# Turning normed tiles with VectorE and a scratch tensor instead of TensorE in a chunk-attention and Fourier-mixing kernel

## The chip, the cores and the metric

The kernel runs on one core of one Trainium2 chip. TensorE (PE in the profile) multiplies, and also transposes by a product with an identity matrix; VectorE (DVE), ScalarE (ACT) and GpSimd (POOL) do elementwise work; the sync engine (SP) issues nearly all DMAs, which 16 DMA engines carry out. The metric is the device time of one execution in microseconds (us). Lower is better.

## The reference

All tensors are fp32. Attention works on chunks of 64 tokens, and its output is the input of a Fourier block with an MLP:

```python
# q, k, v: (8 batches, 8 heads, 576 tokens, 64); chunks of 64 tokens
scores = scale * np.matmul(q_c, k_c.transpose(0, 1, 2, 4, 3))
scores = scores - np.max(scores, axis=-1, keepdims=True)
attn = np.exp(scores)
attn = attn / (np.sum(attn, axis=-1, keepdims=True) + 1e-09)
out = np.matmul(attn, v_c)
# x: (8, 576, 512), the heads side by side
X = np.fft.fft(x, axis=1)
X = np.fft.fft(X, axis=2)
mixed = np.real(X).astype(np.float32)
u = x + mixed
un = (u - mu) / np.sqrt(var + 1e-06)        # mean and variance over the 512
ch = np.maximum(un @ w_ch1, 0.0) @ w_ch2    # 512 -> 2048 -> 512
return (u + ch).astype(np.float32)
```

## The kernel before

**Tiles and groups.** The 8 x 576 tokens are cut into tiles of 128 tokens by 512 features. A batch gives two low tiles (LO) and two high tiles (HI, kept in reversed order, so that the Fourier step can use symmetries), and the middle chunks of two batches share a rest tile (RE). Four tiles make a group: groups 0 to 7 are the batches, group 8 the four rest tiles. The MLP runs over whole groups, one after the other. While the MLP of group g runs, attention and the Fourier step of batch g+1 are woven into it.

**The MLP in two parts.** Groups 0 and 1 multiply by w_ch1 in the plain way. From group 2 on `up_halves` does this product with the seven products of halves of a Strassen scheme, and from group 1 on `down_halves` (from L1067) does so for w_ch2. Sums and differences of weights were made once and lie in DRAM (`s1`, `s2`). The sync queue fetches them as slabs: a slab of w_ch2 is 1 MB, of which three are held in `wb`; a slab of w_ch1 is 256 KB, of which ten are held in `wa`. `fetch(1)` (L930) and `fetch(2)` (L932) issue the next slab into the place that was just read, so each waits until TensorE is done with it.

`down_halves` takes seven passes o = 0 to 6, each over two row blocks r = 0, 1. So there are 14 steps k = 2 o + r. A step is eight fp32 products of 128x128 by 128x256, which the trace shows as 16 records, followed by one evacuation. `fetch(2)` comes after the odd steps, so one slab serves one pass. The results of a group are ready in the last passes: `store(low, ...)` comes in steps 10 and 11, `store(high, ...)` in steps 12 and 13. For an LO tile `store` is one DMA that writes the two chunks of the tile with their rows reversed (L876, access pattern 2x64x512); for an HI tile there are two DMAs of 64 rows (L885).

**The next group's input.** During `down_halves` of group g the four tiles s = 0 to 3 of group g+1 are made ready. `normed(g+1, s)` subtracts the mean and multiplies by the inverse deviation (VectorE, L845) in step 3 + 2s. `turned(g+1, s)` transposes the normed tile `un`, with tokens on the partitions, into 128 columns of `unT`, with features on the partitions. It issues four 128x128 transposes on TensorE into a PSUM tile `pt` (L333), in the middle of step 5 + 2s, and then one copy from PSUM to `unT`: by ScalarE for s = 0 and 2 (L858), by VectorE for s = 1 and 3 (L856). `combined(g+1, q)` then makes the sums that the Strassen scheme needs, with four VectorE additions (L866 to L869), of which the first two give t1 and t2. For q = 0 it needs tiles 0 and 2, in step 9; for q = 1 it needs tiles 1 and 3, in step 11. `up_halves` of the next group begins with the product number 1 (`UP = (1, 0, ...)`), whose moving operand is t2 over the columns of both q.

**What sets the order.** The program is written in a fixed order for each engine (a manual schedule); waits between engines follow from which buffers are read and written. An engine and the sync queue take their instructions strictly in the order written. So a DMA that must wait holds back every later DMA of the sync queue. The DMAs use eight completion semaphores in turn, so that a DMA also waits for the eighth before it. Buffers in a pool are reused in turn; the normed tiles come from three buffers with the tag "o".

Of the kernel before, what the change touches and what calls it, by code (L numbers as in the profile page):

```python
# [8 lines left out]
FP32 = mybir.dt.float32  # L9
# [7 lines left out]
def kernel(  # L17
# [32 lines left out]
    nc = tc.nc  # L50
# [9 lines left out]
    KD = DM // 128  # L60
    KF = DFF // 128
# [5 lines left out]
    G = 2 * NM  # L67
# [4 lines left out]
    one_p = ctx.enter_context(tc.tile_pool(name="one", bufs=1))  # L72
    two_p = ctx.enter_context(tc.tile_pool(name="two", bufs=2))
    three_p = ctx.enter_context(tc.tile_pool(name="three", bufs=3))
# [4 lines left out]
    dram = ctx.enter_context(tc.tile_pool(name="dram", bufs=1, space=bass.MemoryType.DRAM))  # L79
# [19 lines left out]
    NO, HF = 7, KF // 2  # L99
    UP = (1, 0, 2, 3, 4, 6, 5)  # L100
    s1 = dram.tile([HF // 2, NO, 128, 2 * 2 * 128], FP32, name="s1")
    s2 = dram.tile([NO, 128, HF * HM], FP32, name="s2")
    NS1, NS2, Z1, Z2 = 10, 3, 2 * 2 * 128, HF * HM
    slab1 = [wa[:, i * Z1:(i + 1) * Z1].rearrange("p (k r f) -> p k r f", r=2, k=2) for i in range(NS1)]
    slab2 = [wb[:, i * Z2:(i + 1) * Z2].rearrange("p (m e) -> p m e", m=HF) for i in range(NS2)]
# [21 lines left out]
    groups = [[at[what, b, i] for i in range(NM) for what in (LO, HI)] for b in range(B)]  # L127
    rests = [at[RE, b, 0] for b in range(0, B, 2)]
    groups += [rests[i:i + G] for i in range(0, NP, G)]
    NG = len(groups)  # L130
# [198 lines left out]
    def turn(src):  # L329

        pt = ps_t.tile([128, 4, 128], FP32, tag="pt", name="pt")
        for j in range(4):
            nc.tensor.transpose(pt[:, j, :], src(j), ident)  # L333
        return pt
# [489 lines left out]
    uns, unTs = {}, {}  # L824

    def natural(n):

        return xt(n)[:, DM:0:-1] if kind(n) == HI else xt(n)[:, 0:DM]
# [19 lines left out]
    def turned(g, s):  # L848
        if s >= len(groups[g]):
            return  # L850
        if s == 0:
            unTs[g] = one_p.tile([128, KD, G * 128], FP32, tag="unT", name="unT")
        unT, un = unTs[g], uns.pop((g, s))
        pt = turn(lambda j: un[:, j * 128:(j + 1) * 128])
        if s % 2 and g > 1:
            nc.vector.tensor_copy(unT[:, :, s * 128:(s + 1) * 128], pt)  # L856
        else:
            nc.scalar.copy(unT[:, :, s * 128:(s + 1) * 128], pt)  # L858

    def combined(g, q_):  # L860

        unT = unTs[g]
        cl, ch = slice(q_ * 128, (q_ + 1) * 128), slice(256 + q_ * 128, 256 + (q_ + 1) * 128)
        b11, b12, b21, b22 = unT[:, 0:2, cl], unT[:, 0:2, ch], unT[:, 2:4, cl], unT[:, 2:4, ch]
        t1, t2, t4 = (tt[:, o, :, cl] for o in range(3))
        nc.vector.tensor_tensor(out=t1, in0=b12, in1=b11, op=ALU.subtract)  # L866
        nc.vector.tensor_tensor(out=t2, in0=b22, in1=t1, op=ALU.subtract)
        nc.vector.tensor_tensor(out=b12, in0=b22, in1=b12, op=ALU.subtract)
        nc.vector.tensor_tensor(out=t4, in0=b21, in1=t2, op=ALU.subtract)  # L869

    def store(n, o):

        if kind(n) == LO:
            b, c = chunks(n)[0]
            to = out[b, c * CH + 1:c * CH + 129, :].rearrange("(c p) d -> c p d", c=2)
            nc.sync.dma_start(out=to[:, ::-1], in_=o)  # L876
            return
        for h, (b, c) in enumerate(chunks(n)):
            r0, t0 = h * CH, c * CH
            if kind(n) == RE:  # L880
                eng = nc.scalar if n in groups[-1][1::2] and h else nc.sync
                eng.dma_start(out=out[b, t0 + 1:t0 + CH, :], in_=o[r0 + 1:r0 + CH])
                eng.dma_start(out=out[b, 0:1, :], in_=o[r0:r0 + 1])
            else:
                nc.sync.dma_start(out=out[b, t0:t0 + CH, :], in_=o[r0:r0 + CH])  # L885
# [40 lines left out]
    def fetch(which):  # L926
        i = n_slab[which]
        if which == 1 and i < HF // 2 * NO * (NG - first_of[1]):
            pair, o = divmod(i % (HF // 2 * NO), NO)
            nc.sync.dma_start(out=slab1[i % NS1].rearrange("p k r f -> p (k r f)"), in_=s1[pair, UP[o]])  # L930
        elif which == 2 and i < NO * (NG - first_of[2]):
            nc.sync.dma_start(out=slab2[i % NS2].rearrange("p m e -> p (m e)"), in_=s2[i % NO])  # L932
        n_slab[which] = i + 1
# [133 lines left out]
    def down_halves(g, h1):  # L1067
        pas, pbs = {}, {}
        for o in range(NO):
            w = slab2[((g - first_of[2]) * NO + o) % NS2]  # L1070
            for r in range(2):
                cl, ch = slice(r * 128, (r + 1) * 128), slice(256 + r * 128, 256 + (r + 1) * 128)
                low, high = groups[g][r], groups[g][2 + r]
                olow, ohigh = os_[:, 2 * r], os_[:, 2 * r + 1]
                a, b = tmp[:, r, 0], tmp[:, r, 1]
                if o == 0:
                    pas[r] = ps_f.tile([128, 2, 256], FP32, tag="ff", name="pa")
                if o == 2:
                    pbs[r] = ps_f.tile([128, 2, 256], FP32, tag="ff", name="pb")
                dst = (pas, pas, pbs, pbs, pas, pbs, pbs)[o][r][:, (0, 1, 0, 1, 0, 0, 1)[o]]  # L1080
                lhs = (
                    h1[:, 0:HF, cl], ys[:, :, cl], xs[:, :, cl], h1[:, 0:HF, ch],
                    h1[:, HF:KF, cl], ys[:, :, cl], h1[:, HF:KF, ch],
                )[o]
                k = 2 * o + r
                for m in range(HF):
                    if m == HF // 2 and g + 1 < NG and k in range(5, 5 + 2 * G, 2):
                        turned(g + 1, (k - 5) // 2)
                    nc.tensor.matmul(  # L1089
                        out=dst, lhsT=lhs[:, m], rhs=w[:, m],  # L1090
                        start=(o in (0, 2) and m == 0), stop=(m == HF - 1), skip_group_check=True,
                    )
                if o == 0:
                    nc.scalar.copy(a, dst)
                elif o == 1:
                    nc.vector.tensor_tensor(out=b, in0=dst, in1=a, op=ALU.add)
                elif o == 2:
                    nc.vector.tensor_tensor(out=a, in0=dst, in1=b, op=ALU.add)
                elif o == 3:
                    nc.vector.tensor_tensor(out=ohigh[:, HM:DM], in0=dst, in1=ohigh[:, HM:DM], op=ALU.add)  # L1100
                    nc.gpsimd.tensor_tensor(out=olow[:, HM:DM], in0=b, in1=natural(low)[:, HM:DM], op=ALU.add)
                    nc.gpsimd.tensor_tensor(out=ohigh[:, 0:HM], in0=b, in1=natural(high)[:, 0:HM], op=ALU.add)
                elif o == 4:
                    nc.vector.tensor_tensor(out=olow[:, 0:HM], in0=dst, in1=natural(low)[:, 0:HM], op=ALU.add)
                elif o == 5:
                    nc.vector.tensor_tensor(out=olow[:, HM:DM], in0=dst, in1=olow[:, HM:DM], op=ALU.add)
                    store(low, olow)
                else:
                    nc.vector.tensor_tensor(out=ohigh[:, 0:HM], in0=dst, in1=ohigh[:, 0:HM], op=ALU.add)
                    store(high, ohigh)  # L1110
                if g + 1 < NG:
                    for j in range(G):
                        if k == 3 + 2 * j:
                            normed(g + 1, j)
                        if k == 5 + 2 * j and j >= 2:
                            combined(g + 1, j - 2)
                if r == 1:
                    if o == 1:
                        for j in range(0, HF, 2):
                            two = ys[:, j:j + 2]  # L1120
                            nc.gpsimd.tensor_tensor(
                                out=two, in0=h1[:, HF + j:HF + j + 2, lo], in1=two, op=ALU.subtract
                            )
                    if o == 2:
                        for i in range(2):
                            nc.gpsimd.tensor_tensor(
                                out=os_[:, 2 * i + 1, HM:DM], in0=tmp[:, i, 0],
                                in1=natural(groups[g][2 + i])[:, HM:DM], op=ALU.add,
                            )
                    fetch(2)  # L1130
                yield
# [7 lines left out]
    with tc.manual_schedule():  # L1139
# [71 lines left out]
        t = 0  # L1211
# [84 lines left out]
```

## Time and profile before

| | |
|---|---|
| time, median of 3 | 1090.42 us (1089.04 to 1094.13) |
| TensorE busy | 1070.4 us, 98% of the span of 1089.0 us |
| VectorE busy | 577.2 us, 53% |
| ScalarE, GpSimd busy | 299.2 us, 280.3 us |
| DMA | 192.73 MB, 58.4% of 16 engines on the sync queue |
| transposes of normed tiles (L333, pt<-ident,un) | 144 for all 36 tiles |
| `down_halves` of group 7 | about 944 to 987 us |
| `down_halves` of groups 2, 3, 4, 5 | end at about 432, 548, 664, 781 us |

A row of the profile names the line, the engine, the operation and the tiles (out<-in), with shapes and a count, and then busy time and mean duration. fp32 products appear as two records each. Matmuls are pipelined: the start of the next one tells more than the end of the last. "SPq" is the sync queue: its rows are the issues of DMAs, and the time beside them is the time to issue, not to land. When a DMA has landed is told by its semaphore's updates, which the trace holds too.

### The profile page before, as it was taken

Reading aid. Unit: us, or ns where it says so; the run is one execution under the profiler, and the core shown is the slowest. Engines: PE = TensorE matmul, PEld = TensorE weight load, DVE = VectorE, ACT = ScalarE, POOL = GpSimd, SP = SyncE. Lnnn points to the kernel's source line nnn. Section 1 sums busy time; section 2 is a strip of 40 time slices with the busy share of each in tenths; the row PEclk is TensorE's granted clock in tenths of the full one; section 3 lists DMA queues with packets and bytes.
Section 4 is the critical chain, followed back from the end, with each engine's and each line's share of the span. In section 5 each row is a group of like instructions: output and inputs, shape, how many; then the busy total and the mean of one; then the engine's idle time right before and its main releaser. Section 6 shows DMA issues by size and latency. Waiting matters only on the chain.

```text
span 1089.0 us, 18837 instructions
## 1 busy us (share of the span) xinstructions
PE 1070.4 (98%) x7018; PEld 848.7 (78%) x7018; DVE 577.2 (53%) x1258; ACT 299.2 (27%) x730; POOL 280.3 (26%) x403
## 2 busy tenths in 40 slices
PE   8999999999999999999999999999999999999998
PEld 6644454446888888888888888888888888888887
DVE  4899987314566355663556455735663534323411
ACT  4788453222113310322022212321133103101300
POOL 4301002444405140153114220514051401210140
PEclk9999999999999999999999999999999999999999
DMA  7777556679575637692668357854653455446232
GB/s 167 224 222 175 158 162 227 171 239 308 178 203 167 198 136 206 189 255 95 191 184 253 124 165 223 206 170 152 197 185 90 147 190 163 120 154 211 78 116 78
DMA packets 147970, 192.73 MB, mean 177 GB/s; under 512 B 66126, under 2 KB 104014, under 8 KB 140712
## 3 DMA queue, kind: packets, MB, share of 16 engines
q1 hardware_dynamic: 145620, 190.20, 58.4%
q8 instruction: 56, 0.92, 0.4%
q0 software_dynamic: 512, 0.68, 0.3%
q10 hardware_dynamic: 1748, 0.66, 0.2%
q14 instruction: 34, 0.28, 0.1%
HBM read 167.22 MB, written 24.12 MB: 176 GB/s over the span
## 4 chain that ended last, share of the span: by engine, by line
PE 89%; DVE 4%; ACT 2%; DMA 2%; SPq 2%; issue 1%; POOL 0%; DVEq 0%; ACTq 0%
PE pb L1089 20%; PE pa L1040 17%; PE pa L1089 15%; PE pb L1040 13%; PE up L973 4%; PE up L953 3%; PE pt L333 3%; PE dn L994 3%; PE mix L700 2%; PE sc L384 2%; PE more_z L652 2%; PE xp L432 2%; PE z L652 1%; PE idle L1167 1%; DMA xall<-in_moe_w_ch_dram 1%; SPq L195 1%
## 5 line engine op out<-in xcount | busy, mean ns | idle before, releaser
L1040 PE MATMUL pa<-unT,wa 128*128 128x256 f32 x672 | 159.5, 380 | 1.1 <-DVE wa L1048 1.1
L1040 PEld LDWEIGHTS pa<-unT,wa 128*128 128x128 f32 x672 | 126.5, 190 | 18.9 <-DVE wa L1048 1.5
L941 POOL TENSOR_TENSOR h<-h 128x256 f32<-128x256 f32 x64 | 55.7, 877 | 269.5 <-PE pb L1040 150.5
L1089 PE MATMUL pa<-wb,h 128*128 128x256 f32 x512 | 115.6, 380 | 0.0
L1089 PE MATMUL pb<-wb,h 128*128 128x256 f32 x512 | 114.9, 379 | 0.0
L1040 PE MATMUL pb<-wa 128*128 128x256 f32 x448 | 106.6, 381 | 0.0
L1089 PEld LDWEIGHTS pa<-wb,h 128*128 128x128 f32 x512 | 96.1, 190 | 13.5 <-issue 0.5
L1089 PEld LDWEIGHTS pb<-wb,h 128*128 128x128 f32 x512 | 96.3, 190 | 12.6
L1040 PEld LDWEIGHTS pb<-wa 128*128 128x128 f32 x448 | 84.2, 190 | 11.6 <-DVE h L1056 0.2
L994 PE MATMUL dn<-wb,h 128*128 128x512 f32 x128 | 58.4, 605 | 0.9 <-ACT h L964 0.9
L1046 DVE TENSOR_TENSOR wa<-pb,wa 128x256 f32<-128x256 f32 x56 | 23.5, 423 | 65.5 <-ACT wa L1045 65.5
L1089 PE MATMUL pb<-wb,yall 128*128 128x256 f32 x256 | 58.2, 381 | 0.0
L1089 PE MATMUL pa<-wb,yall 128*128 128x256 f32 x256 | 57.9, 380 | 0.0
L1089 PE MATMUL pb<-wb 128*128 128x256 f32 x256 | 57.7, 379 | 0.0
L973 PE MATMUL up<-unT,wa 128*128 128x512 f32 x128 | 56.8, 596 | 0.0
L1045 ACT COPY wa<-pa 128x256 f32<-128x256 f32 x56 | 20.8, 372 | 125.1 <-PE pa L1040 125.1
L1040 PE MATMUL pa<-wa 128*128 128x256 f32 x224 | 53.5, 382 | 0.0
L717 POOL TENSOR_TENSOR xall<-y,xall 128x513 f32<-128x513 f32 x14 | 21.3, 1518 | 125.3 <-DVE y L711 125.3
L1040 PE MATMUL pb<-unT,wa 128*128 128x256 f32 x224 | 52.9, 379 | 0.0
L1089 PEld LDWEIGHTS pa<-wb,yall 128*128 128x128 f32 x256 | 47.7, 190 | 6.4
L1089 PEld LDWEIGHTS pb<-wb,yall 128*128 128x128 f32 x256 | 47.7, 190 | 6.3
L1089 PEld LDWEIGHTS pb<-wb 128*128 128x128 f32 x256 | 47.6, 190 | 5.9
(250 smaller groups left out, 1685.0 us busy)
## 6 DMA issues: line engine op xcount, KB each, us to landing
wb<-s SPq DMA_DIRECT2D x56, 1024.0 KB
wa<-s SPq DMA_DIRECT2D x196, 256.0 KB
xall<-in_moe_w_ch_dram SPq DMA_DIRECT2D x22, 512.0 KB
q<-in_q_dram SPq DMA_DIRECT2D x96, 112.0 KB
k<-in_k_dram SPq DMA_DIRECT2D x96, 112.0 KB
v<-in_v_dram SPq DMA_DIRECT2D x124, 64.0 KB
yall<-in_moe_w_ch_dram SPq DMA_DIRECT2D x10, 512.0 KB
s<-wb SPq DMA_DIRECT2D x20, 256.0 KB
```

The source lines that it names most:

```text
L333: nc.tensor.transpose(pt[:, j, :], src(j), ident)
L384: nc.tensor.matmul(out=sc[t0:t0 + CH, e, j * CH:(j + 1) * CH], lhsT=a[r0:r0 + D, 2 * j + c, 0:CH], rhs=b[r0:r0 + D, 2 * j + c, 0:CH], star ...
L432: nc.tensor.matmul(out=xp[0][e][t0:t0 + CH, j * DV:(j + 1) * DV], lhsT=a[r0:r0 + CH, j, t0:t0 + CH], rhs=b[r0:r0 + CH, c, j, :], start=Tru ...
L652: nc.tensor.matmul(out=out_, lhsT=lhsT[p], rhs=tk[p, i, T // 2 if T != 5 else 0, cols], start=start, stop=stop, skip_group_check=True,)
L700: nc.tensor.matmul(out=mix[:, cols], lhsT=zt[:, T], rhs=tab, start=(T == 0), stop=(T == 3), skip_group_check=True,)
L941: nc.gpsimd.tensor_tensor(out=h1[:, m, hi], in0=h1[:, m, lo], in1=h1[:, m, hi], op=ALU.subtract)
L953: nc.tensor.matmul(out=up, lhsT=w1[:, kk, m * 128:(m + 1) * 128], rhs=unT[:, kk], start=(kk == 0), stop=(kk == KD - 1), skip_group_check=True,
L973: nc.tensor.matmul(out=up, lhsT=w1[:, kk, m * 128:(m + 1) * 128], rhs=unT[:, kk], start=(kk == 0), stop=(kk == KD - 1),)
L994: nc.tensor.matmul(out=dn, lhsT=h1[:, m, s * 128:(s + 1) * 128], rhs=w2[:, m, :], start=(m == 0), stop=(m == KF - 1),)
L1040: nc.tensor.matmul(out=dst, lhsT=w[:, kk, r], rhs=rhs[o][:, kk], start=(o in (0, 1) and kk == 0), stop=(kk == 1), skip_group_check=True,)
L1046: nc.vector.tensor_tensor(out=b, in0=pbs[r][:, 0], in1=a, op=ALU.add)
L1089: nc.tensor.matmul(out=dst, lhsT=lhs[:, m], rhs=w[:, m], start=(o in (0, 2) and m == 0), stop=(m == HF - 1), skip_group_check=True,)
```

## The change

From the third group on (groups 2 to 8; the first to be made ready inside `down_halves`) a normed tile no longer goes to TensorE. VectorE transposes it in 32x32 blocks (`flipped`), in the same step as `normed`. What is then missing is the order of the blocks: the rows of a block lie on the right 32 partitions only within the block. `sent` writes the blocks to a scratch tensor in DRAM with four DMAs, one for each set of 32 partitions, at the places where they belong, in runs of 32 elements (128 bytes). `fetched` reads the 128 columns of the tile back with one DMA into `unT`, in runs of 512 bytes. There are two scratch tensors, used by groups in turn. `combined` moves to steps 11 and 12. The purpose is to take the transposes off TensorE, and the evacuations of PSUM off ScalarE and VectorE. The computed values are the same.

```diff
+    un_d = [dram.tile([128, KD, G * 128], FP32, name=f"un_d{i}") for i in range(2)]
...
+    blocks = {}
+
+    def flipped(g, s):
+        if s >= len(groups[g]):
+            return
+        un = uns.pop((g, s))
+        t = three_p.tile([128, KF, 32], FP32, tag="o", name="blocks")
+        nc.vector.transpose(out=t, in_=un.rearrange("p (b f) -> p b f", f=32))
+        blocks[g, s] = t
+
+    def sent(g, s):
+        if s >= len(groups[g]):
+            return
+        t = blocks.pop((g, s))
+        to = un_d[g % 2].rearrange("(a f) k t -> f k a t", a=4)
+        for i in range(4):
+            nc.sync.dma_start(
+                out=to[:, :, :, s * 128 + 32 * i:s * 128 + 32 * (i + 1)],
+                in_=t[32 * i:32 * (i + 1)].rearrange("f (k a) t -> f k a t", a=4),
+            )
+
+    def fetched(g, s):
+        if s >= len(groups[g]):
+            return
+        if s == 0:
+            unTs[g] = one_p.tile([128, KD, G * 128], FP32, tag="unT", name="unT")
+        cols = slice(s * 128, (s + 1) * 128)
+        nc.sync.dma_start(out=unTs[g][:, :, cols], in_=un_d[g % 2][:, :, cols])
...
                 for m in range(HF):
-                    if m == HF // 2 and g + 1 < NG and k in range(5, 5 + 2 * G, 2):
-                        turned(g + 1, (k - 5) // 2)
                     nc.tensor.matmul(
...
                         if k == 3 + 2 * j:
                             normed(g + 1, j)
-                        if k == 5 + 2 * j and j >= 2:
+                            flipped(g + 1, j)
+                        if k == 4 + 2 * j:
+                            sent(g + 1, j)
+                        if k == 5 + 2 * j:
+                            fetched(g + 1, j)
+                        if k == 6 + 2 * j + (j == 2) and j >= 2:
                             combined(g + 1, j - 2)
```

## The prediction

> **What bounds the kernel now.** I read the page first, then who waits for whom, then the end of the second part of group 7 closely, because the change works in that part (groups count from 0; the parts touched are those of groups 1 to 7) and group 7 has no attention woven in. The first part of the page:
>
> ```profile
> PE 1070.4 (98%) x7018; PEld 848.7 (78%) x7018; DVE 577.2 (53%) x1258; ACT 299.2 (27%) x730; POOL 280.3 (26%) x403
> ...
> PEclk9999999999999999999999999999999999999999
> ```
>
> TensorE has work for 98% of the span at full clock. The waits of TensorE, longest first, are about a microsecond each, and none is for a DMA:
>
> ```profile
> PE sc L384 <- ACT kT L372: 1.7, 2, 1.0
> PE sc L384 <- DVE rd L445: 1.4, 1, 1.4
> PE idle L1167 <- DVE more_v L1148: 1.2, 1, 1.2
> PE mix L700 <- ACT zr L681: 1.1, 1, 1.1
> PE pa L1040 <- DVE wa L1048: 1.1, 1, 1.1
> ```
>
> So work taken from TensorE shortens the span by its own length, unless something new makes TensorE wait. The timeline of TensorE at the end of group 7 shows what is taken (columns: start, time to the end of the last):
>
> ```profile
> 973.10 5.34 PE L1089 MATMUL pb<-wb,yall 128*128 128x256 f32 x24
> 978.28 0.60 PE L333 MATMUL pt<-ident,un 128*128 128x128 f32 x4
> 978.72 1.89 PE L1089 MATMUL pb<-wb,yall 128*128 128x256 f32 x8
> 980.45 7.07 PE L1089 MATMUL pb<-wb,h 128*128 128x256 f32 x32
> 987.36 1.89 PE L1040 MATMUL pb<-wa 128*128 128x256 f32 x8
> ```
>
> The four transposes of one tile hold up the next product from 978.28 to 978.72: 0.44 us. A step k of `down_halves` is 16 records at 0.216 us, 3.45 us. The sync queue and the DMA engines at the same place:
>
> ```profile
> 977.28 0.56 SPq L876 DMA_DIRECT2D out_dram<-wb  x1
> 981.17 1.14 SPq L885 DMA_DIRECT2D out_dram<-wb  x2
> 982.40 0.54 SPq L932 DMA_DIRECT2D wb<-s  x1
> ```
>
> ```profile
> core 0: us, PE busy (x) PEld busy (x) DVE busy (x) ACT busy (x) POOL busy (x), PEclk, DMA share, GB/s
> 978.50:981.50 3.00, 3.00 (x17) 2.69 (x16) 1.45 (x3) 0.00 (x0) 0.00 (x0) 1.00 0.13 32
> 976.00:978.00 2.00, 2.00 (x11) 1.77 (x10) 0.42 (x1) 0.00 (x0) 0.00 (x0) 1.00 0.70 295
> ```
>
> While a weight slab lands (976 to 978) the engines move 295 GB/s. Then only the store of L876 is under way, and the share is 0.13, two engines of 16. Its 256 KB were issued at 977.28 and landed at 985.10, by the semaphore records: 7.8 us, where a slab of four times the size, issued at 965.95, landed at 970.71 (4.8 us).
>
> **What the skill says.** The Trainium skill, "DMA: Bandwidth & Descriptors", section "Why a DMA increments its semaphore by 16 and not by 1": a copy is spread over the largest number of engines, up to 16, that divides the slowest dimension of both sides, and takes the lowest-numbered ones. The store of a low tile has a slowest dimension of 2, so two engines: the 0.13 agrees. The same page, "Queues, rings and completion order": on each engine the descriptors of one queue are consumed in order. The trace agrees: in group 2 the q loads issued at 420.86 to 422.2, just after such a store (issued 419.84, landed 427.74), landed at 428.44 to 430.45; others took 2.3 us (404.44 to 406.77). The same page, "Specifications": below 512 B a transfer loses the line rate to read-modify-write. No 128-byte write to DRAM is in this trace.
>
> **Part by part.**
>
> Removed: 28 tiles (7 groups of 4) times four transposes, 28 x 0.44 = 12.3 us of TensorE, all on the path. Also 28 evacuations (14 of 0.69 us on VectorE, 14 of 0.58 us on ScalarE), worth nothing: both engines idle between steps here (11.6 and 1.5 us busy of the last 44 us of group 7).
>
> Added on VectorE: 28 block transposes. The nearest row, that of L352, takes 1.1 us for 128x512. VectorE gains 31 - 10 = 21 us of work beside TensorE. It comes after the evacuation of its step, and the next is 3.45 us later: hidden, 0.
>
> Added on the sync queue, for each tile: four sends and one fetch. A send has 512 pieces of 128 B; the loads of v, with 256 pieces, take 0.65 us to issue, the first q loads with 1024 take 0.85; I take 0.65, so 2.6 us for four. Each of the 16 engines gets 128 pieces. For a piece the packet records bound it: 128-byte packets (224, from SBUF to SBUF) take 11 ns, 256-byte ones 18 ns, 1024-byte ones 46 ns. Because of the loss below 512 B I take 20 ns: 2.6 us an engine; 11 gives 1.4, 46 gives 5.9. The fetch is 256 KB in 512-byte pieces; a 256-KB slab of w1 issued at 371.06 landed at 373.57, so 2.5 us; I take 2.6.
>
> The new wait: the fetch stands on the sync queue until the sends have landed. Behind it are the next weight slab, stores and loads of q and k. For the first three tiles this costs nothing: sent after the slab of the step (issued at 958.6, landed at 963.4), the second tile lands about 965.5, when the next slab may be asked for anyway (965.95), and a slab is used two passes, some 14 us, after its issue while it needs 4.8.
>
> The fourth tile is different. Its normalization is at k = 9, its send at k = 10, and in the program order of step 10 `store(low)` comes first. In the order of the changed program the send does follow the L876 store in all seven groups. Worked in group 7, with three sets of transposes (1.3 us) gone by then:
>
> - the store issues at 977.28 - 1.33 = 975.95, lands 7.8 later at 983.8;
> - the sends issue from 976.6 to 979.2, but on the store's two engines their pieces follow it: 983.3 + 2.6, with 0.4 for the receipt, 986.3;
> - the fetch issues then and lands 2.6 later, 988.9;
> - `combined` needs two additions of 0.42 us until t2 is there: 989.9. The first product of `up_halves` reads t2 (UP begins with 1).
>
> TensorE without a wait would be there at 987.36 - 4 x 0.44 = 985.6. It waits 4.3 to 4.4 us. Before, t2 was ready at 982, 5 us early.
>
> In group 3 the same sum goes: store 536.32 - 1.33, landed 542.8, sends 545.4, fetch 548.1, t2 549.0. Attention products give TensorE 1.5 us more to do: 548.02 - 1.76 = 546.3. Wait 2.9. In groups 2 and 4 four q loads come between sends and fetch and hold the two engines 0.7 us each: the fetch lands at 433.2, t2 at 434.1, against 431.54 - 1.76 = 429.8. Wait 4.3.
>
> Sum: groups 1, 3, 5 at 2.9, groups 2 and 4 at 4.3, groups 6 and 7 at 4.4: 26.1 us of wait. 26.1 - 12.3 = +13.8, so 1090.4 + 13.8 = 1104.
>
> VectorE waits too, at `combined` of k = 12; behind it stand the last evacuation, softmax and the k transposes. Their products are asked for 5 us or more into the next `up_halves`, which is itself late, and the sums in PSUM need no answer before. The loads of k stand some 4 us longer on the sync queue. In the trace VectorE waits 21.4 us for k loads in all and TensorE never does. I take 0.
>
> **Rivals.**
>
> 1. All hidden: the send is not held by the store, or fast enough. Then 1090.4 - 12.3 = 1078. For it: TensorE is the bound. Against it: with no time at all for the small pieces group 7 has store landed 983.8, fetch 986.4, t2 987.4, still 1.8 us late.
> 2. Gain and wait cancel: pieces at 11 ns and a fetch of 2.2 take 1.6 us off every wait, 26.1 - 11 = 15, so +3: 1088 to 1094.
> 3. Small writes are dear, and the scratch traffic becomes the bound: at 60 ns a piece the sends take 7.7 us an engine, more than a pass of 7.3 us with its slab of 4.5; the last wait grows by 5.1: 26.1 + 36 - 12 = +50, 1140. For it: the read-modify-write. Against it: the stores of 1024 and 2048 B show packets hardly slower than loads.
> 4. The clock drops in the new pauses. "TensorE: Matmul & The Clock Gate", "Part 1: The HAM clock gate", says that an idle window of about 3.4 us halves the clock. Before, no pause is long enough to show it. An estimate from that page: in half the groups 2 us more, +7: 1111. It lies in the range.
>
> **Numbers.** Forecast with rival 4 (1095 to 1118): 0.56. Rival 1: 0.13. Rival 2: 0.16. Rival 3: 0.15. Rival 2 reaches to both sides of the bound of 0.5% (1085 to 1096) only a little: same 0.15, faster 0.13, slower 0.72. The range takes in most of rival 2 and the cheaper half of rival 3 (46 ns, 1128): 1087 to 1130.
>
> **What would show it.** Right: no rows of transposes of `un` in groups 2 to 8 and TensorE about 12 us less busy; the waits of TensorE led by `up_halves` (pb or its weight load) for VectorE's `combined`, seven times, 2 to 5 us; VectorE's `combined` waiting for the DMA of unT; the sync queue's fetch waiting for the DMA of the scratch. Wrong: seven short pauses or none, the sends landing with the other engines rather than after the store; or pauses inside the 14 steps, for slabs, which would be rival 3. My forecast falls if a 128-byte piece costs far from 20 ns, or if the store leaves the engines sooner than its landing says.

## The result, and the profile after

The kernel after takes 1139.68 us (median, 1139.17 to 1141.52), the kernel before beside it 1089.73 us: a ratio of 1.0452, 95% interval 1.0429 to 1.0475. The forecast was 1104 us with a range to 1130. The direction was right, and the size was missed by 36 us.

The first part of the page of after:

```profile
PE 1075.8 (95%) x6906; PEld 848.9 (75%) x6906; DVE 591.8 (52%) x1272; ACT 292.6 (26%) x716; POOL 280.1 (25%) x403
...
PEclk9999999999989998999899998999899989998999
```

TensorE has 112 records fewer and yet is busy 5 us longer than before: seven slices show a digit 8 in the clock row, which had only nines. A product at half clock is busy twice as long. The waits of TensorE (us in total, times, longest):

```profile
PE pb L1070 <- DVE wa L897: 23.4, 4, 6.5
PE sc L385 <- DVE kT L353: 20.1, 3, 7.3
```

Seven waits, one at the end of each `down_halves` from group 1 on, 43.5 us in all. Four are those that the prediction named (t2 of `combined`, L897). The three in groups 1, 3 and 5 wait for something that it did not name: the transposes of k (L353).

Group 7, which the prediction worked out. The timeline of TensorE, and then of VectorE:

```profile
1032.92 3.78 PE L1070 MATMUL pb<-wa 128*128 128x256 f32 x8 [5.62 <-DVE wa L897]
1036.49 1.91 PE L1070 MATMUL pa<-unT,wa 128*128 128x256 f32 x4
```

```profile
1023.88 0.42 DVE L1137 TENSOR_TENSOR wb<-pb,wb 128x256 f32<-128x256 f32 x1 [1.50 <-PE pb L1117]
1031.98 0.43 DVE L896 TENSOR_TENSOR wa<-unT 128x256 f32<-128x256 f32 x1 [7.67 <-DMA unT<-un_d]
1032.44 0.42 DVE L897 TENSOR_TENSOR wa<-unT,wa 128x256 f32<-128x256 f32 x1
```

TensorE stands 5.62 us, VectorE 7.67 us for the fetch. The sync queue there (times to issue):

```profile
1015.73 0.56 SPq L888 DMA_DIRECT2D unT<-un_d  x1
1016.34 0.62 SPq L962 DMA_DIRECT2D wb<-s  x1
1017.50 0.58 SPq L906 DMA_DIRECT2D out_dram<-wb  x1
1018.13 7.50 SPq L877 DMA_DIRECT2D un_d<-blocks  x4
...
1028.92 0.59 SPq L888 DMA_DIRECT2D unT<-un_d  x1
```

By the semaphore records the slab (L962) landed at 1022.08, the low-tile store (L906) at 1027.25, the four sends from 1027.65 to 1028.78, the fetch at 1031.95. So the chain is the one that was forecast: store, sends, fetch, t2.

The clock does not come back at once. The table of stretches (PE busy and its records; PEclk is the third number from the right):

```profile
1028.00:1030.00 2.00, 0.00 (x0) 0.00 (x0) 0.00 (x0) 0.00 (x0) 0.00 (x0) 1.00 0.49 109
1030.00:1034.00 4.00, 1.08 (x3) 0.91 (x4) 1.86 (x5) 0.00 (x0) 0.00 (x0) 0.71 0.87 311
1034.00:1036.00 2.00, 2.00 (x6) 1.62 (x5) 0.00 (x0) 0.00 (x0) 0.00 (x0) 0.50 0.52 132
1036.00:1038.00 2.00, 2.00 (x6) 1.58 (x5) 0.00 (x0) 0.00 (x0) 0.00 (x0) 0.50 0.91 274
1038.00:1040.00 2.00, 2.00 (x9) 1.70 (x9) 0.55 (x2) 0.74 (x2) 0.00 (x0) 0.88 0.97 388
1040.00:1042.00 2.00, 2.00 (x11) 1.79 (x10) 1.13 (x3) 0.00 (x0) 0.00 (x0) 1.00 0.70 229
```

At clock 0.50, 2 us hold 6 records in place of 11. The half clock starts before the pause ends and lasts 6.83 us here. Over the seven pauses these stretches are 6.83 us long five times and 10.24 us twice; some 35.8 us of them fall on products, and half of that, 17.9 us, is lost.

How long such a stretch lasts can be worked out from the traces. Thirteen of the fourteen (before, after and the experiments, all but 10) hold such stretches between 100 us and the end. In each trace they begin and end on one fixed beat of 3.41 us. Cut the time at that beat and take TensorE's idle share in each piece, with the ends of products as the profile models them. The clock fell after each of the 47 pieces that were idle for 56% or more, after none of the 3,657 with 50% or less, and after 5 of the 11 in between. It came back after each of the 52 pieces with 15% idle or less, and after none of the 45 with 18% or more. So the half clock lasts through the rest of the piece in which the pause ends, and, when more than 15% of that piece was idle, through one more. Two pieces or three is then a matter of where the pause begins: group 2's, from 436.49, left its first piece (to 437.75) idle for 37%, and the clock fell one piece later; group 3's, from 558.70, left its first piece (to 560.63) idle for 57%, and the clock fell at once. An estimate from these figures: a single pause of less than 1.7 us does not lower the clock, and one of more than 3.8 us always does.

Sum, with the 12.3 us of the forecast: 43.5 of pauses + 17.9 of clock - 12.3 of transposes gone = +49.1; the profiled spans differ by 1137.6 - 1089.0 = 48.6. (Experiment 8 puts the gain nearer 10; the sum then overshoots by 2 to 3 us, of which 1.1 is a wait of the kernel before, for L1048, that is gone.)

Group 3 stands for groups 1, 3 and 5, where attention is woven in. The chain of work there, in order of time (start, duration):

```profile
547.14 5.80 DMA wb<-s
552.94 0.02 issue
552.95 1.44 SPq L877
554.39 0.04 issue
554.44 5.76 DMA un_d<-blocks
...
560.25 3.10 DMA unT<-un_d
563.36 0.02 issue
563.38 0.44 DVE wa L896
...
564.51 0.42 DVE wa L899
564.93 1.00 DVE kT L353
565.93 0.04 issue
565.98 1.13 PE sc L385 x32
567.11 3.71 PE pb L1070 x8
```

The score products sc come ahead of the first product with t2 in TensorE's order, and need kT. Its transpose stands on VectorE behind all four additions of `combined`, and these behind the fetch. Before, the same transpose ran at 543.49, ahead of need. So TensorE waits for t2 and then for L898, L899 and kT, with sc still to do.

### The profile page after: what moved, and what is told of

It reads as the page before. It is cut to its first block, busy times and chain, and to the rows that moved or that the text cites. A ratio compares the mean times of both kernels' runs of the same rounds, so it can differ in the third digit from the quotient of the medians.

```text
span 1137.6 us, 18806 instructions
## 1 busy us (share of the span) xinstructions
PE 1075.8 (95%) x6906; PEld 848.9 (75%) x6906; DVE 591.8 (52%) x1272; ACT 292.6 (26%) x716; POOL 280.1 (25%) x403
## 4 chain that ended last, share of the span: by engine, by line
PE 75%; DMA 10%; SPq 5%; DVE 5%; ACT 2%; issue 1%; POOL 1%; DVEq 0%; ACTq 0%; POOLq 0%
PE pa L1070 17%; PE pb L1070 14%; PE pa L1117 13%; PE pb L1117 11%; PE up L1003 4%; DMA un_d<-blocks 4%; PE up L983 3%; SPq L877 3%; PE dn L1024 3%; DMA wb<-s 3%; DMA unT<-un_d 2%; PE mix L701 2%; PE more_z L653 2%; PE sc L385 1%; PE z L653 1%; PE pt L334 1%
## 5 line engine op out<-in xcount | busy, mean ns | idle before, releaser
L1070 PE MATMUL pa<-unT,wa 128*128 128x256 f32 x672 | 163.1, 387 | 0.0
L1070 PEld LDWEIGHTS pa<-unT,wa 128*128 128x128 f32 x672 | 130.4, 196 | 19.0
L1070 PE MATMUL pb<-wa 128*128 128x256 f32 x448 | 119.0, 413 | 23.4 <-DVE wa L897 23.4
L1070 PEld LDWEIGHTS pb<-wa 128*128 128x128 f32 x448 | 91.7, 208 | 38.6 <-DVE wa L897 24.4
L718 POOL TENSOR_TENSOR xall<-y,xall 128x513 f32<-128x513 f32 x14 | 24.0, 1711 | 124.3 <-DVE y L712 114.3
```

The costliest lines, as they stand in the source:

```text
L718: eng.tensor_tensor(out=x[:, 0:w], in0=y[:, 0:w], in1=x[:, 0:w], op=ALU.add)
L1070: nc.tensor.matmul(out=dst, lhsT=w[:, kk, r], rhs=rhs[o][:, kk], start=(o in (0, 1) and kk == 0), stop=(kk == 1), skip_group_check=True,)
```

## The experiments

All times have the kernel before beside them on the same chip; its medians lie between 1089 and 1091 us. Diffs are against the kernel after, unless they say otherwise.

**1. Undo the fourth tile alone.** Tiles 0 to 2 of a group go through memory, the fourth is turned by TensorE again.

```diff
+                    if m == HF // 2 and g + 1 < NG and k == 3 + 2 * G:
+                        turned(g + 1, G - 1)
...
-                            flipped(g + 1, j)
-                        if k == 4 + 2 * j:
+                            if j < G - 1:
+                                flipped(g + 1, j)
+                        if k == 4 + 2 * j and j < G - 1:
                             sent(g + 1, j)
-                        if k == 5 + 2 * j:
+                        if k == 5 + 2 * j and j < G - 1:
```

> The fourth tile of each group (s = 3) goes back to TensorE and ScalarE/VectorE; the first three keep VectorE and the scratch tensor. Theory (the loss sits in the fourth tile alone: its sends land behind the store of the low tile, TensorE pauses some 6 us and then runs at half clock): the seven pauses go, 21 of 28 turns stay off TensorE, 1090 - 21 x 0.44 = 1081 us (1078 to 1086). Rival 'small pieces' (28 tiles of 128-byte writes load the DMA engines all along) and rival 'VectorE' (28 block transposes hold up its other work): three quarters of the loss stay, about 1127 us.

Measured: 1092.05 us, ratio 1.0018 (1.0005 to 1.0031). The seven pauses are gone, so the loss of the whole change is the fourth tile's. But the 9 us of gain that three tiles should bring did not come either. In its place are short pauses inside the next `up_halves` (2.63, 1.65, 0.67 and 1.33 us), and the longest of them has 3.41 us of half clock behind it. Two of its waits:

```profile
PE pa L1070 <- DVE wa L1078: 3.5, 3, 1.7
PE pb L1070 <- DMA wa<-s: 2.6, 1, 2.6
```

So the first three tiles are not free: TensorE now waits for a slab of w_ch1, which no wait of the kernel before does.

**2. Keep the clock up through the pauses.** Eight products of constants at the end of step 13, whose results nobody reads; this adds work to TensorE.

```diff
+                if k == 13 and g + 1 < NG:
+                    pt = ps_t.tile([128, 512], FP32, tag="pt", name="filler")
+                    for _ in range(8):
+                        nc.tensor.matmul(
+                            out=pt[:, 0:NQ], lhsT=warm[:, 0:128], rhs=warm[:, 0:NQ], start=True, stop=True
+                        )
```

> The changed kernel with eight products of constants (289 columns, about 4 us of TensorE) at the end of step 13, in front of the place where TensorE pauses; their results go unused. Theory (pause 43.5 us in all, and some 18 us more [...]): the pauses shrink by the filler to 1 to 3 us, the clock stays full, the end of each pause stays where it was: 1140 - 18 = 1122 us (1117 to 1127). Rival (the half clock in the records costs little, the whole loss is waiting): 1138 to 1141 us.

Measured: 1122.26 us, ratio 1.0288 (1.0264 to 1.0312). The page's clock row:

```profile
PEclk9999999999999999999999999999999999999999
```

17.4 us come back. The seven fillers take 4.06 us each and the seven pauses that are left 14.9 us in all, together 43.4 us in place of 43.5, so the chain to t2 is as long as it was. What came back is the clock's share of the loss, and it agrees with the 17.9 us worked out from the trace.

**3. Put the stores later.** All stores of steps 10 and 11 are issued behind the fetch of the fourth tile.

```diff
-                    store(low, olow)
+                    late.append((low, olow))
...
+                if k == 11:
+                    for args in late:
+                        store(*args)
```

> The changed kernel with the stores of the low tiles of steps 10 and 11 issued after the fetch of the fourth tile instead of before its sends. Theory (the store, on two engines, stands in front of the sends): sends land behind the slab alone, about 4 us earlier, the fetch too; pauses fall to 0.4 us in four groups and about 1.7 in the three where the k transpose stands behind combined on VectorE; no half clock: 1090 + 7 - 12 = 1084 us (1080 to 1092). Rival 'small pieces': the sends still take long, above 1125 us.

Measured: 1118.43 us, ratio 1.0253 (1.0228 to 1.0279), far from the 1084 expected. The pauses at the ends of `down_halves` fell to 1.9 us or less, as they should, and others came in the next `up_halves`:

```profile
PE pb L1070 <- DMA wa<-s: 11.9, 7, 3.0
PE pa L1070 <- DVE h L1086: 5.7, 3, 2.8
PE pa L1070 <- DVE wa L1078: 5.6, 3, 1.9
```

The gain was given back later: the stores, now back to back, held slabs of w_ch1 and loads instead (VectorE waited 34.5 us for loads of k, in after 17.7), and five times 3.41 us of half clock followed. My theory of a mere order on the queue fell here in part: whatever stands behind the stores is late.

**4. Large pieces in place of 128-byte ones.** The blocks are sent as rows of 2 KB and fetched in rows of 2 KB. They are not put in order, so unT holds other values.

```diff
-        to = un_d[g % 2].rearrange("(a f) k t -> f k a t", a=4)
+        plain = un_d[g % 2].rearrange("p k t -> (p k t)").rearrange("(s p f) -> s p f", s=G, p=128)
...
-                out=to[:, :, :, s * 128 + 32 * i:s * 128 + 32 * (i + 1)],
-                in_=t[32 * i:32 * (i + 1)].rearrange("f (k a) t -> f k a t", a=4),
+                out=plain[s, 32 * i:32 * (i + 1)],
+                in_=t[32 * i:32 * (i + 1)].rearrange("f b t -> f (b t)"),
...
-        nc.sync.dma_start(out=unTs[g][:, :, cols], in_=un_d[g % 2][:, :, cols])
+        plain = un_d[g % 2].rearrange("p k t -> (p k t)").rearrange("(s p k t) -> s p k t", s=G, p=128, k=KD)
+        nc.sync.dma_start(out=unTs[g][:, :, cols], in_=plain[s])
```

> The changed kernel with the same bytes sent in rows of 2 KB (and fetched in rows of 2 KB) instead of pieces of 128 B; the blocks are not put in order, so unT holds other values. Theory: the sends' own part of each pause is about 1.5 us of it, of which some 0.8 goes, and a little of the fetch: 1127 to 1136 us, the pauses stay. Rival 'small pieces': most of the loss goes, below 1100 us.

Measured: 1117.03 us, ratio 1.0243 (1.0221 to 1.0264). Better than expected: the pauses sum to 25.4 us in place of 43.5. In group 7 the store landed 8.2 us after its issue (999.81 to 1008.02) where after had 9.75, because a faster send of the third tile let the slab ahead of it go earlier; and the fetch landed 4.2 us after the store where after had 4.7. Summed over the seven groups, the low-tile store waited for its turn on the queue for 1.6 us where after had 10.0, it then took 56.5 us where after had 59.4, and the last send landed 5.3 us behind it where after had 10.8. Small pieces, of sends and fetch together, cost about 2.6 us of each pause, and more than half of the loss is there without them.

**5. Another order of the same work.** The fourth tile is sent ahead of the slab of step 9; its fetch comes ahead of the low-tile store; the fetches of the first three come behind the slab.

```diff
-                    store(low, olow)
+                    if not (k == 10 and g + 1 < NG):
+                        store(low, olow)
...
-                        if k == 4 + 2 * j:
+                        if k == 4 + 2 * j - (j == 3):
                             sent(g + 1, j)
-                        if k == 5 + 2 * j:
+                        if k == 10 and j == 3:
                             fetched(g + 1, j)
+                            store(low, olow)
+                            fetch(2)
...
-                    fetch(2)
+                    if not (k == 9 and g + 1 < NG):
+                        fetch(2)
+                    if g + 1 < NG and k in (5, 7, 9):
+                        fetched(g + 1, (k - 5) // 2)
```

> Nothing of the work is left out; only the order on the sync queue changes. The fourth tile is sent at the end of step 9, ahead of the slab; at step 10 the fetch of the fourth tile goes out first and the low-tile store (L906) behind it; the fetches of the first three tiles go out behind the slab's fetch. Theory (the pause is the store with the slab in front of it, and the half clock that follows): the fetch of the fourth tile is asked about 3 us after step 9, so the pauses end, the clock stays up, and the 12.3 us of TensorE come through: 1082 us (1078 to 1092, the upper end if slabs of w_ch1 come late in the next up_halves as they did with later stores). Rival (the two engines of the store are simply given too much work in this stretch, whatever the order): pauses only move, 1110 us or more.

Measured: 1115.53 us, ratio 1.0223 (1.0206 to 1.0239). The rival's number came true: the pauses move. None waits for `combined` any more, and 26 us of pauses stand in `up_halves`. The longest, in the `up_halves` of group 6, on TensorE and then on VectorE:

```profile
817.27 3.78 PE L1070 MATMUL pa<-unT,wa 128*128 128x256 f32 x8 [4.52 <-DVE h L1086]
```

```profile
815.88 1.08 DVE L353 STREAM_TRANSPOSE kT<-k 128x512 f32<-128x512 f32 x1 [5.10 <-DMA k<-in_k_dram]
816.82 0.73 DVE L1086 TENSOR_TENSOR h<-pa,wa 128x256 f32<-128x256 f32 x2
```

VectorE stands 5.10 us for a load of k; behind it stands the sum L1086, and behind that TensorE. The loads of k were issued up to 808.34 and landed up to 815.86, after the second low-tile store (803.87 to 814.03).

**6. The store on another queue.** ScalarE's queue issues the low-tile stores.

```diff
-    def store(n, o):
+    def store(n, o, early=False):
...
-            nc.sync.dma_start(out=to[:, ::-1], in_=o)
+            (nc.scalar if early else nc.sync).dma_start(out=to[:, ::-1], in_=o)
...
-                    store(low, olow)
+                    store(low, olow, True)
```

> The low-tile stores of steps 10 and 11 are asked by ScalarE's queue; nothing else is changed. Theory (the sends and the fetch wait behind the store because they are in order on one queue): the pauses fall by about 4 us each, to about 2, the clock holds, 1093 us (1086 to 1102). Rival (the engines that write the low tile are overloaded, whichever queue asks): the sends' and the fetch's pieces on those two engines come behind the store all the same, 1130 to 1140 us.

Measured: 1175.16 us, ratio 1.0774 (1.0742 to 1.0806): worse than both. TensorE's pauses reach 14.9 us. The sync queue in group 7:

```profile
1053.88 0.56 SPq L888 DMA_DIRECT2D unT<-un_d  x1
1054.54 0.56 SPq L962 DMA_DIRECT2D wb<-s  x1
1055.20 12.69 SPq L877 DMA_DIRECT2D un_d<-blocks  x4
```

Two things show. The first send, issued at 1055.20 on a queue where the store is not, landed at 1065.78, just ahead of the store (1054.14 to 1065.95). By the semaphore records 14 of its 16 engines were done by 1060.21; the last two were done at 1065.62 and 1065.78, and the store's two at 1065.85 and 1065.95. So the two engines are shared, whoever asks. The Trainium skill says so in "DMA: Bandwidth & Descriptors", "Issuing engines are not separate DMA queues": DMAs of any issuing engine run on the same 16 engines and interleave. And the second send was issued only at 1065.97, when the store had landed: its completion semaphore was the store's, the eighth before it. The second is an effect of the eight semaphores, so the run does not tell how long the pauses would be without it.

**7. The same edit on the kernel before**, as its control.

> Control for the run before it: the kernel before, with its low-tile stores asked by ScalarE's queue. Nothing in the kernel before waits for that store, so both theories expect no effect: 1088 to 1092 us.

Measured: 1095.35 us, ratio 1.0041 (1.0024 to 1.0058). That is 3 us above the range, and a small part of 6's loss.

**8. What the removal alone is worth.** VectorE copies the normed tile to unT; nothing is turned, sent or fetched.

```diff
-        t = three_p.tile([128, KF, 32], FP32, tag="o", name="blocks")
-        nc.vector.transpose(out=t, in_=un.rearrange("p (b f) -> p b f", f=32))
-        blocks[g, s] = t
+        if s == 0:
+            unTs[g] = one_p.tile([128, KD, G * 128], FP32, tag="unT", name="unT")
+        nc.vector.tensor_copy(unTs[g][:, :, s * 128:(s + 1) * 128], un.rearrange("p (k t) -> p k t", k=KD))
...
-                        if k == 4 + 2 * j:
-                            sent(g + 1, j)
-                        if k == 5 + 2 * j:
-                            fetched(g + 1, j)
```

> Leaves the turning out from the third group on: VectorE copies the normed tile into unT as it is, with no blocks, sends or fetches, so that unT holds other values. What is left is the removal of 28 turnings from TensorE alone, with a VectorE copy of the same size as the block transpose. Theory: 28 x 0.44 = 12.3 us saved and no pause: 1078 us (1076 to 1081). Rival (TensorE waits elsewhere for what the saving brings forward, slabs or VectorE): 1084 to 1090 us.

Measured: 1083.16 us, ratio 0.9926 (0.9907 to 0.9944), so 8 us (6 to 10) and not 12.3. The trace puts the shortfall in two places: `down_halves` of group 7 (937.25 to 987.36 in before) is shorter by 1.76 us, exactly four times 0.44, but the seven of groups 1 to 7 together by 10.2, the others gaining 0.97 to 1.75 each; and the `up_halves` that follow differ by up to 1.4 us either way. The profiled execution, at 1081.15 us, was the fastest of the four.

**9. The store on all engines.** The low tile's rows are written in natural order, which leaves out their reversal; the bytes are the same.

```diff
-            nc.sync.dma_start(out=to[:, ::-1], in_=o)
+            nc.sync.dma_start(out=out[b, c * CH + 1:c * CH + 129, :], in_=o)
```

> Leaves out that the rows of a low tile are written in reversed order: the store L906 writes the same 256 KB in natural order, so its pieces spread over all DMA engines where the reversed store used two; nothing else is changed. Theory (the store on two engines is what the sends wait for): in group 7 the store would land about 1 us after the slab (1023 in place of 1027.25), the sends near 1024, the fetch near 1027, and step 13 ends at 1027.3, so that pauses of 1 to 2 us are left, no half clock: 1087 us (1080 to 1094). Rival (the chain of sends of 128-byte pieces and fetch is too long by itself, whatever stands ahead of it): 1110 us or more.

Measured: 1098.71 us, ratio 1.0089 (1.0059 to 1.0119); 41 of the 50 us are gone. Its waits of TensorE:

```profile
PE pb L1070 <- DVE wa L897: 12.5, 4, 5.8
PE sc L385 <- DVE kT L353: 6.3, 3, 2.5
```

18.8 us in place of 43.5. In group 7 the store, issued at 985.73 behind the same slab, landed at 992.08 (6.35 us, the slab itself at 991.43), and the sends 1.5 us after it. The rule of the slowest dimension that the prediction quoted is borne out: with 128 rows 16 engines tell of its landing, with 2x64 in after two do. Left are pauses of 1.6 to 3.4 us, and one of 5.8 in group 4, and behind three of them 13.7 us of half clock, which the theory had excluded; its 1087 was 12 us too good. So sends and fetch are too long even without the two engines, which is the rival's argument, though its number did not come.

**10. The same edit on the kernel before**, as its control.

> Control for the run before it: the kernel before with the same natural order of the low tile's rows, which leaves out their reversal. Nothing on TensorE waits for that store in the kernel before: 1088 to 1091 us.

Measured: 1086.75 us, ratio 0.9967 (0.9954 to 0.998). That is below the range: the reversed stores cost the kernel before some 3 us. Against this control 9 is slower by 12 us, so about 38 of the 50 us go with the two engines.

**11. Only the first two tiles.** They are sent at steps 4 and 6, before any store; tiles 2 and 3 are turned by TensorE.

```diff
+                    if m == HF // 2 and g + 1 < NG and k in (9, 11):
+                        turned(g + 1, (k - 5) // 2)
...
-                            flipped(g + 1, j)
-                        if k == 4 + 2 * j:
+                            if j < 2:
+                                flipped(g + 1, j)
+                        if k == 4 + 2 * j and j < 2:
                             sent(g + 1, j)
-                        if k == 5 + 2 * j:
+                        if k == 5 + 2 * j and j < 2:
                             fetched(g + 1, j)
-                        if k == 6 + 2 * j + (j == 2) and j >= 2:
+                        if k == 5 + 2 * j and j >= 2:
```

> Only the first two tiles of each group go through VectorE and memory; the third and fourth are turned by TensorE as before. Their traffic is done before the first low-tile store. Theory (only traffic asked beside or behind the two low-tile stores costs anything): 14 x 0.44 = 6.2 us saved, no new pauses: 1085 us (1081 to 1088). Rival (the first tiles' traffic also delays slabs and loads that are needed later): 1090 us or more.

Measured: 1084.99 us, ratio 0.9955 (0.9939 to 0.9971). As expected, and faster than both kernels, by 3 to 7 us against before. Its longest wait of TensorE for a DMA of this stretch:

```profile
PE pa L1070 <- DMA wa<-s: 1.5, 1, 1.5
```

Between this run and 1 stand the third tile, whose sends go out before the low-tile store, and the later place of `combined` (steps 11 and 12, here 9 and 11). The third tile off TensorE should bring 3 us; with both, 1 is 7 us slower (1092.05 against 1084.99).

**12. `combined` one step later on VectorE.**

```diff
-                        if k == 6 + 2 * j + (j == 2) and j >= 2:
+                        if k == 7 + 2 * j and j >= 2:
```

> The last combined (L896 to L899) is put behind step 13 instead of step 12 on VectorE, so that the k transposes of groups 3, 5 and 7's predecessors (the odd ones) no longer stand behind its wait for the fetch. Theory (in groups 1, 3 and 5 sc waits only because kT stands behind combined, which costs the 1.0 us of the kT transpose and the 1.1 us of sc in each): the pauses before sc end, pauses before pb L1070 some 1.5 us shorter take their place, and with the half clock that is 4 to 6 us in all: 1135 us (1131 to 1139). Rival (the wait is the fetch alone and VectorE's order costs nothing): 1140 us, or a little more.

Measured: 1128.27 us, ratio 1.0363 (1.0338 to 1.0388), 11 us better than after; more than the 4 to 6 expected. All seven waits are now of one kind:

```profile
PE pb L1070 <- DVE wa L897: 35.8, 7, 6.7
```

The three pauses of groups 1, 3 and 5 fell from 20.1 to 13.1 us in sum, the other four from 23.4 to 22.7. VectorE's order was worth 2.3 us on the average of the three. The pauses fell by 7.7 us, and the profiled execution, the slowest of its four at 1132.34 us, is 7.4 us shorter than that of after; the half clock on products is no less in it (37.8 us against 35.8). The other three, without a profile, took 1127.3 to 1128.7 us at a mean clock of 0.985, where the profiled one had 0.977 and after 0.974 to 0.977. So the rest of the 11 us is likely the clock's, which no profile shows.

## Why the prediction missed

| term | predicted, us | measured, us |
|---|---|---|
| transposes off TensorE | -12.3 | -10.2 in the `down_halves` of 8, -8 (6 to 10) in its time |
| pauses in groups 1, 3, 5 | 3 x 2.9 = 8.7 | 20.1 |
| pauses in groups 2, 4 | 2 x 4.3 = 8.6 | 13.0 |
| pauses in groups 6, 7 | 2 x 4.4 = 8.8 | 10.4 |
| half clock | 0 (7 as rival 4) | 17.9 by the trace, 17.4 by 2 |

- **The mechanism was right.** In all seven groups, by the semaphore records, 14 of the 16 engines were done with the first send of the fourth tile 2.4 to 5.0 us before the low-tile store had landed, and the last one 0.4 us after it; TensorE waits through fetch and `combined`. 1 shows that it is the fourth tile, 9 that most of it is the two engines.
- **The failed step with the largest part is the clock, left out of the forecast.** "In half the groups 2 us more" stood beside the sum, as rival 4, with nothing in the sum itself. All seven pauses, 4.8 to 7.3 us long, brought the half clock, at 2.6 us each. By the estimate above even the forecast's own pauses of 4.3 and 4.4 us, in four groups, would each have brought it. The Trainium skill ("TensorE: Matmul & The Clock Gate", "Part 1: The HAM clock gate") gives one idle window of about 3.4 us to halve the clock and one busy window to restore it. The traces agree on the unit (3.41 us) but not on the idle one: a unit that is idle for 56% is enough. So "Before, no pause is long enough to show it" was a wrong reading too: the trace of before has 3.41 us at half clock from 153.63 on, behind waits of 1.12 and 0.82 us that follow closely on each other, and the unit ahead of it was idle for 51%.
- **The second failed step: VectorE's queue, "I take 0".** That their products are asked for "5 us or more into the next `up_halves`" was wrong for k: sc stands ahead of the first product with t2. The pauses of groups 1, 3 and 5 were mis-sized by 11.4 of the 17.4 us that are missing. For group 3, whose own figures give a wait of 2.7 us (549.0 - 546.3) and not 2.9: t2 was ready 1.8 us later than forecast relative to TensorE's work, L898, L899 and kT took 1.7 us more, and sc, which the forecast had done before the wait, 1.1 us. 12 shows the last two, with 2.3 us a group.
- **The third failed step: "for the first three tiles this costs nothing".** In groups 2 and 4 the fetch of the third tile held the sync queue until its sends had landed (issued at 422.81, landed at 422.73; 669.38 and 669.32); in groups 1, 3 and 5 four loads of k stood in front of it as well. What stood behind it went out late, the low-tile store too: in groups 1 to 5 it was issued 1.2, 1.7, 2.9, 2.5 and 1.8 us after the addition on VectorE that makes it ready (L1134). In groups 6 and 7, and in all seven before, it was 0.03 us. Group 2, on VectorE and then on the sync queue:

```profile
424.70 0.42 DVE L1134 TENSOR_TENSOR wb<-pb,wb 128x256 f32<-128x256 f32 x1 [0.72 <-PE pb L1117]
```

```profile
422.81 0.56 SPq L888 DMA_DIRECT2D unT<-un_d  x1
423.48 0.56 SPq L962 DMA_DIRECT2D wb<-s  x1
424.14 2.65 SPq L219 DMA_DIRECT2D v<-in_v_dram  x4
426.83 0.61 SPq L906 DMA_DIRECT2D out_dram<-wb  x1
```

The pauses of groups 2 and 4 were 6.5 and 6.4 us for the 4.3 of the forecast. Of that excess, 2.2 and 2.1 us, the late store accounts for most.
- **The store's landing, 7.8 us, was too short.** It was read where the slab ahead landed 0.8 us after the store's issue. In after it took 8.0 to 8.6 us in groups 1 to 6, and 9.75 in group 7, where the slab landed 4.6 us after the store's issue. The fetch behind it, taken as 2.6 us, took 3.0 there.
- **The sends' pieces were priced too dear.** 57,568 packets of 128 bytes, all but 224 of them the sends', took 13 ns at the median, where 20 was taken; the last send landed 1.5 us after the store, where the forecast has 2.5 (983.8 to 986.3). Their issue, taken as 2.6 us, took 7.5 in group 7, but behind the store that was hidden.
- **The block transpose** took 0.71 us (1.1 taken), and hid as said.
- **Rival 3** came near in number (1140), for another reason: its price of 60 ns a piece was 13. What small pieces cost, 22.6 us by 4, comes in good part from the queue they hold up, as the sums there show.

The parts are not additive: undoing the clock's share gives 17, VectorE's order 11, the small pieces 23, the two-engine store 41 (38 against its control), and the fourth tile 48 us. A shorter pause can also leave less half clock: 3.41 us behind three of the seven in 4, none behind four of the seven in 9.

What stays open is how much of the short waits in experiments 1, 3 and 5 is the load on the two engines and how much the sync queue that stands; 9 changes both at once. Nor is it settled why the pause of group 4 in 9 is 5.8 us long, or why the issue of a send takes up to 3.3 us while the store is under way.

## What to carry to other kernels

Before traffic is added beside TensorE, look for DMAs of few engines in the same stretch: all that is asked behind them is as late as they are, on any queue, and reordering only chooses who waits. Follow each new wait on an in-order engine through everything queued behind it, until the engine that sets the end asks for one of those things. And price a pause of TensorE of 4 us or more at its length plus the half clock behind it, here 2.1 to 3.0 us each; a shorter one, down to 2 us, can cost that too, by where it falls.

## What the runs showed of the hardware that was not expected

- The issue of a send of the first three tiles takes 0.57 to 0.78 us in most cases. For the fourth tiles of after, with the store under way, the issue of single sends took up to 3.3 us (in group 7 0.6, 3.0, 2.4 and 1.4; with rows of 2 KB, in 4, the four together 2.0).
- Packets of 128 bytes, the sends' to DRAM, took 13 ns, and packets of 512 bytes, the fetches' from DRAM, 27 ns: about half the rate for a quarter of the size.
- The clock fell to half after pieces of 3.41 us that were idle for 56% or more, and came back after the first with 15% idle or less; pauses of 4.8 to 7.3 us brought 6.83 or 10.24 us of it.
- A store of 256 KB behind a 1-MB slab takes 9.75 us on two engines and 6.35 on all of them; in the second case it lands 0.65 us after the slab.
- While the store was under way, 14 of a send's 16 engines were done 5.3 us before the other two (group 7 of after: by 1022.26, then 1027.59 and 1027.65).
